# Reading every matmul's moving operand alternately from its two halves, in a float32r attention and gated-MLP kernel

## The chip, the cores and the metric

The kernel runs on one core of one Trainium2 chip. The metric is device time in microseconds, the median over runs; lower is better.

## The reference

Four sequences of 3008 tokens pass through an attention without softmax, whose result is the input of a gated MLP. Cut to what matters (the MLP's weights are float64, all else float32):

```python
scores = (1 / S) * np.matmul(z, z.transpose(0, 2, 1))      # z: 4 x 3008 x 64
attn   = np.maximum(scores, 0.0) ** 2
x      = (u * np.matmul(attn, v)).reshape(B * S, D)         # u, v: 4 x 3008 x 256
gate   = 1.0 / (1.0 + np.exp(-(x @ w_gate)))                # 256 x 1536
out    = (gate * (x @ w_val)) @ w_out                       # 1536 x 256
```

## The kernel before

All matmuls but 18 (a warm-up in bf16, L456) are in float32r: four bytes an element. To keep float32 precision each operand is held as a rounded high part and the remainder (`ah`/`al`, `vh`/`vl`, `xh`/`xl`, `hh`/`hl`, `wgv_h`/`wgv_l`, `wo_h`/`wo_l`), and a product is three matmuls into one PSUM tile: high by high, high by low, low by high. The scores do it with two, since `zP` and `zQ` hold high and low stacked over the 128 partitions.

The queries of a sequence are cut into six chunks of 512 columns, the last of 448 (3008 = 5 x 512 + 448); a chunk's columns are the moving operand of every matmul that belongs to it. The keys go in 12 pairs of 128. A step is one (sequence, chunk, pair). In a step TensorE works, in this order, on

- `pe_scores` (L260, L261) of the next step: 4 matmuls into `sc`; for a key block whose scores were computed earlier, the transposed block comes back from DRAM instead (`load_back`) and there are none;
- `pe_pv` (L330, L331, L333): 12 matmuls into `acc`, which grows over the 12 steps of a chunk;
- `pe_out` (L401 to L403): 6 matmuls into `oacc`, for the MLP of the chunk before, two feature blocks back;
- `pe_gv` (L358 to L360): 12 matmuls into `gv`, gate and value of one feature block, for the chunk before.

The step order is written out by hand in one loop (under `manual_schedule`), and every engine runs its part in that order. PSUM is full: `sc`, `gv`, `acc` and `oacc` are single tiles of two banks each.

Who reads PSUM: the Relu of `post_scores` on ScalarE (ACT, L271, followed by a square in SBUF); the Sigmoid of `gate` on ACT (L369) and the product of gate and value on VectorE (DVE, L370); `make_x` on DVE (L338), once a chunk, which multiplies `acc` by the transposed `u`; and `finish` on DVE (L408), which transposes the output in blocks of 32 by 32. Everything else that prepares a moving operand (`split`, `split_h`, `split_x`, the casts of `post_scores`) works from SBUF to SBUF.

Before the change all of these patterns are plain: a matmul reads its n columns in order, one after the other, and so do those that read its product.

Of the kernel before, what the change touches and what calls it, by code (L numbers as in the profile page):

```python
# [13 lines left out]
AF = mybir.ActivationFunctionType  # L14
ALU = mybir.AluOpType
# [13 lines left out]
def kernel(  # L29
# [19 lines left out]
    nc = tc.nc  # L49
    P = 128  # L50
# [6 lines left out]
    NF = DFF // P  # L57
    NB = D // P
    TAIL = S - (2 * NPAIR - 1) * P
    assert D == 256 and DQ == 64 and NF == NPAIR and TAIL == 64 and S % 32 == 0  # L60
    scale = 1.0 / S

    def chunk(c):
        return min(CH, S - c * CH)
# [11 lines left out]
    def f32(ap):  # L76
        return ap.bitcast(F32)


    def kept(b, c, e):  # L80
        return e > c and (b, c) not in ((0, 0), (0, 1))


    def back(b, c, k):
        return kept(b, k // 2, c)
# [159 lines left out]
    def early(b, c):  # L245
        return (b, c) == (0, 0)
# [4 lines left out]
    def pe_scores(b, c, k):  # L251
        if back(b, c, k):
            return
        n = chunk(c)
        sc = ps.tile([P, 2, CH], F32, tag="gv" if early(b, c) and k % 2 else "sc", name="sc")
        kP = z_t[b, k // 2][0]
        qP, qQ = z_t[b, c]
        for j in range(2):
            o = (k % 2) * 256 + j * P
            nc.tensor.matmul(sc[:, j, 0:n], kP[:, o : o + P], qP[:, 0:n], start=True, stop=False)  # L260
            nc.tensor.matmul(sc[:, j, 0:n], kP[:, o : o + P], qQ[:, 0:n], start=False, stop=True)  # L261
        sc_t[b, c, k] = sc

    def post_scores(b, c, k):
        n = chunk(c)
        sc = sc_t.pop((b, c, k), None)
        if back(b, c, k):
            r = r_t.pop((b, c, k))
        else:
            r = two.tile([P, 2, CH], F32, tag="r", name="r")  # L270
            nc.scalar.activation(r[:, :, 0:n], sc[:, :, 0:n], AF.Relu, scale=scale)  # L271
            nc.scalar.activation(r[:, :, 0:n], r[:, :, 0:n], AF.Square)  # L272
        if early(b, c) and k % 3 == 2:
            ah = one.tile([P, 2, CH], F32R, tag="xh", name="ah")
            al = one.tile([P, 2, CH], F32R, tag="xl", name="al")
        else:
            ah = two.tile([P, 2, CH], F32R, tag="ah", name="ah")
            al = two.tile([P, 2, CH], F32R, tag="al", name="al")
        if back(b, c, k) or (b, c) == (0, 1) or (early(b, c) and k % 2):
            nc.scalar.activation(ah[:, :, 0:n], r[:, :, 0:n], AF.Copy)  # L280
        else:
            nc.vector.tensor_copy(ah[:, :, 0:n], r[:, :, 0:n])  # L282
        nc.vector.tensor_tensor(al[:, :, 0:n], r[:, :, 0:n], f32(ah[:, :, 0:n]), op=ALU.subtract)  # L283
        a_t[b, c, k] = ah, al
        r_t[b, c, k] = r
# [30 lines left out]
    def pe_pv(b, c, k):  # L316
        n = chunk(c)
        if k == 0:
            acc_t[b, c] = ps.tile(
                [P, NB, CH], F32, tag="oacc" if early(b, c) else "acc", name="acc"  # L320
            )
        acc = acc_t[b, c]
        ah, al = a_t.pop((b, c, k))
        vh, vl = v_t[b, k]
        for j in range(2):
            last = k == NPAIR - 1 and j == 1
            for d in range(NB):
                ds = slice(d * P, (d + 1) * P)
                o = acc[:, d, 0:n]
                nc.tensor.matmul(o, vh[:, j, ds], ah[:, j, 0:n], start=(k == 0 and j == 0), stop=False)  # L330
                nc.tensor.matmul(o, vh[:, j, ds], al[:, j, 0:n], start=False, stop=last)  # L331
                if not last:
                    nc.tensor.matmul(o, vl[:, j, ds], ah[:, j, 0:n], start=False, stop=False)  # L333

    def make_x(b, c):
        n = chunk(c)
        acc, ut = acc_t.pop((b, c)), u_t[b, c]
        nc.vector.tensor_tensor(ut[:, :, 0:n], acc[:, :, 0:n], ut[:, :, 0:n], op=ALU.mult)  # L338

    def split_x(b, c):  # L340
        n = chunk(c)
# [6 lines left out]
    gv_t, h_t, oacc_t = {}, {}, {}  # L348

    def pe_gv(b, c, f, tag="gv"):  # L350
        n = chunk(c)
        gv = ps.tile([P, 2, CH], F32, tag=tag, name="gv")
        xh, xl = x_t[b, c]
        for i in range(2):
            o = gv[:, i, 0:n]
            for d in range(NB):
                wh, wl = wgv_h[:, f, i, d, :], wgv_l[:, f, i, d, :]
                nc.tensor.matmul(o, wh, xh[:, d, 0:n], start=(d == 0), stop=False)  # L358
                nc.tensor.matmul(o, wh, xl[:, d, 0:n], start=False, stop=False)  # L359
                nc.tensor.matmul(o, wl, xh[:, d, 0:n], start=False, stop=(d == NB - 1))  # L360
        gv_t[b, c, f] = gv

    g_t = {}
# [1 line left out]
    def gate(b, c, f):  # L365
        n = chunk(c)
        gv = gv_t.pop((b, c, f))
        g = one.tile([P, CH], F32, tag="g", name="g")
        nc.scalar.activation(g[:, 0:n], gv[:, 0, 0:n], AF.Sigmoid)  # L369
        nc.vector.tensor_tensor(g[:, 0:n], gv[:, 1, 0:n], g[:, 0:n], op=ALU.mult)  # L370
        g_t[b, c, f] = g


# [11 lines left out]
    def pe_out(b, c, f):  # L385
        if f == 0:
            t = ps.tile([P, NB, CH], F32, tag="oacc", name="oacc")
            oacc_t[b, c] = [t[:, h] for h in range(NB)]
        for h in range(NB):
            pe_out_half(b, c, f, h)  # L390
        if f == NF - 1:
            osb = two.tile([P, NB, CH // 32, 32], F32, tag="osb", name="osb")
            for h in range(NB):
                finish(b, c, h, osb[:, h])

    def pe_out_half(b, c, f, h):
        n = chunk(c)
        hh, hl = h_t[b, c, f]
        wh, wl = (w[:, f, h * P : (h + 1) * P] for w in (wo_h, wo_l))
        o = oacc_t[b, c][h][:, 0:n]  # L400
        nc.tensor.matmul(o, wh, hh[:, 0:n], start=(f == 0), stop=False)  # L401
        nc.tensor.matmul(o, wh, hl[:, 0:n], start=False, stop=False)  # L402
        nc.tensor.matmul(o, wl, hh[:, 0:n], start=False, stop=(f == NF - 1))  # L403

    def finish(b, c, h, osb):
        n = chunk(c)
        rows = out[b * S + c * CH : b * S + c * CH + n, :]
        nc.vector.transpose(  # L408
            out=osb[:, 0 : n // 32, :].rearrange("p T d -> p (T d)"),
            in_=oacc_t[b, c][h][:, 0:n],  # L410
        )
        for g in range(4):
            d0 = h * P + 32 * g
            nc.sync.dma_start(
                rows[:, d0 : d0 + 32].rearrange("(T p) d -> p T d", p=32),
                osb[32 * g : 32 * g + 32, 0 : n // 32, :],
            )
# [26 lines left out]
    with tc.manual_schedule():  # L444
# [19 lines left out]
        load_v(0, 1)  # L464
        keep_warm(14)
        pe_scores(*steps[0])
        turn_z(0, 1)
        prep_z(0, 1)
        load_z(0, 3)
        post_scores(*steps[0])  # L470
        pe_scores(*steps[1])
        prep_v(0, 0)
        load_v(0, 2)
        post_scores(*steps[1])
        prep_v(0, 1)
        load_v(0, 3)
# [6 lines left out]
        for g, (b, c, k) in enumerate(steps):  # L483
# [3 lines left out]
            if nxt:  # L487
                pe_scores(*nxt)
            if m1:
                gate(*m1)  # L490
            if k == 0 and C > 0:
                split_x(*chunks[C - 1])
            if nxt:
                post_scores(*nxt)
# [14 lines left out]
            if nxt:  # L509
                turn(*nxt)  # L510
            pe_pv(b, c, k)
            if k == (9 if C < 2 else 6):
                load_u(b, c)
            if k == (10 if C < 2 else 8):
                prep_u(b, c)
            if k == NPAIR - 1:
                make_x(b, c)
# [3 lines left out]
            if C > 0:  # L521
                m1 = (*chunks[C - 1], k)
                pe_gv(*m1)
# [16 lines left out]

        last = chunks[-1]
        gate(*m1)
        split_x(*last)
        split_h(*m1)
# [3 lines left out]
        def out_half(f, h):  # L548
            if f == 0:
                t = ps.tile([P, CH], F32, tag=("oacc", "acc")[h], name="oacc")  # L550
                oacc_t.setdefault(last, []).append(t)
            pe_out_half(*last, f, h)
            if f == NF - 1:
                finish(*last, h, two.tile([P, CH // 32, 32], F32, tag="osb", name="osb"))

        for f in range(NF):
            pe_gv(*last, f, tag=("sc", "gv")[f % 2])
            if m1:
                gate(*m1)
                split_h(*m1)  # L560
            if m2:
                if m2[:2] == last:
                    out_half(m2[2], 0)
                else:
                    pe_out(*m2)
            m1, m2 = (*last, f), m1
# [37 lines left out]
```

## Time and profile before

| | |
|---|---|
| median of 3 runs | 2133.43 us (2132.82 to 2134.42) |
| span of the profiled execution | 2132.2 us |
| PE (TensorE matmul) busy | 2103.2 us, 99%, 9354 matmuls |
| PEld (weight loads, beside PE) | 1758.8 us, 82% |
| DVE busy | 1176.6 us, 55% |
| ACT busy | 900.8 us, 42% |
| DMA | 159.86 MB, mean 75 GB/s |
| mean granted TensorE clock | 0.995 of full |

The profiled execution's own time is read as its span; the median of the runs lies 1.2 us above it. A matmul's duration in these rows runs from its start to the end of its drain and overlaps the next one, so the rate of TensorE is read from the distance between starts, or from a long stretch and the count of matmuls in it. A row's count stands behind an x; "idle" and the releaser behind it tell what an engine waited for.

### The profile page before, as it was taken

To read this page: it belongs to the slowest core of one execution; us is meant where nothing else is said; L and a number is where in the kernel's file an instruction comes from. 1 tells how busy PE (TensorE), PEld (TensorE's weight loads), DVE (VectorE), ACT (ScalarE), POOL (GpSimd) and SP (SyncE) were. 2 spreads that over 40 slices of the span, in tenths; PEclk is the share of its full clock that TensorE was granted. 3 is DMA by queue.
4 is the path that set the end of the run, shared out by engine and by line. 5 is a ranking of instruction groups with operands and counts; after the bars stand their busy time and mean duration, and the time that the engine had idled before them with its cause. 6 is when DMAs were issued, how large, how long until landed. Compare 5 with 4: busy or idle time off the path is not lost.

```text
span 2132.2 us, 24546 instructions
## 1 busy us (share of the span) xinstructions
PE 2103.2 (99%) x9354; PEld 1758.8 (82%) x9354; DVE 1176.6 (55%) x1557; ACT 900.8 (42%) x1202; POOL 68.9 (3%) x57
## 2 busy tenths in 40 slices
PE   7799999999999999999999999999999999999998
PEld 5588888888888888888888888888888888888888
DVE  6886545455655464544665645445466565453543
ACT  6674434344444433334544433334444434343332
POOL 2100000001000000001100000000110000000000
PEclk9899999999999999999999999999999999999999
DMA  4321312234434242425253525142535242432311
GB/s 123 97 67 23 67 40 37 60 78 107 78 75 72 65 97 53 104 48 149 70 88 62 100 41 117 34 111 60 140 67 97 46 99 50 97 67 70 88 35 19
DMA packets 689910, 159.86 MB, mean 75 GB/s; under 512 B 640768, under 2 KB 668416, under 8 KB 689792
## 3 DMA queue, kind: packets, MB, share of 16 engines
q1 hardware_dynamic: 689792, 158.30, 34.1%
q8 instruction: 73, 1.20, 0.2%
q14 instruction: 45, 0.37, 0.1%
HBM read 88.74 MB, written 63.44 MB: 71 GB/s over the span
## 4 chain that ended last, share of the span: by engine, by line
PE 95%; DVE 2%; ACT 1%; DMA 1%; issue 0%; SPq 0%; POOL 0%; DVEq 0%; ACTq 0%
PE gv L359 12%; PE gv L360 12%; PE gv L358 12%; PE acc L330 11%; PE acc L331 11%; PE acc L333 11%; PE oacc L402 6%; PE oacc L403 6%; PE oacc L401 6%; PE sc L261 4%; PE sc L260 4%; DMA wraw<-in_moe_w_val_dram 1%; DVE al L283 0%; DVE wb L139 0%; DVE wa L135 0%
## 5 line engine op out<-in xcount | busy, mean ns | idle before, releaser
L369 ACT ACTIVATE g<-gv 128x512 f32<-128x512 f32 (+1 forms) x288 | 169.4, 588 | 1022.9 <-PE gv L360 1003.3
L370 DVE TENSOR_TENSOR g<-gv,g 128x512 f32<-128x512 f32 (+1 forms) x288 | 195.7, 680 | 570.0 <-ACT g L369 569.8
L331 PE MATMUL acc<-al,vh 128*128 128x512 f32 (+1 forms) x1152 | 446.7, 388 | 5.0 <-DVE al L283 4.9
L358 PE MATMUL gv<-xh,wgv_h 128*128 128x512 f32 (+1 forms) x1152 | 444.9, 386 | 4.2 <-ACT xh L94 4.2
L330 PE MATMUL acc<-ah,vh 128*128 128x512 f32 (+1 forms) x1152 | 446.1, 387 | 2.9 <-ACT vh L212 1.5
L359 PE MATMUL gv<-xl,wgv_h 128*128 128x512 f32 (+1 forms) x1152 | 444.6, 386 | 1.1 <-DVE xl L95 1.1
L360 PE MATMUL gv<-xh,wgv_l 128*128 128x512 f32 (+1 forms) x1152 | 444.4, 386 | 0.0
L333 PE MATMUL acc<-ah,vl 128*128 128x512 f32 (+1 forms) x1056 | 408.7, 387 | 1.3 <-POOL vl L95 1.3
L283 DVE TENSOR_TENSOR al<-r,ah 128x1024 fp32r<-128x1024 f32 (+1 forms) x288 | 351.4, 1220 | 42.3 <-ACT ah L280 33.0
L282 DVE CAST ah<-r 128x1024 fp32r<-128x1024 f32 (+1 forms) x168 | 115.8, 690 | 274.8 <-ACT r L272 274.8
L331 PEld LDWEIGHTS acc<-al,vh 128*128 128x128 f32 x1152 | 217.5, 189 | 49.4 <-DVE al L283 8.1
L330 PEld LDWEIGHTS acc<-ah,vh 128*128 128x128 f32 x1152 | 217.4, 189 | 46.2 <-ACT vh L212 1.9
L358 PEld LDWEIGHTS gv<-xh,wgv_h 128*128 128x128 f32 x1152 | 216.8, 188 | 45.8 <-ACT xh L94 5.0
L359 PEld LDWEIGHTS gv<-xl,wgv_h 128*128 128x128 f32 x1152 | 216.8, 188 | 42.2 <-DVE xl L95 1.9
L360 PEld LDWEIGHTS gv<-xh,wgv_l 128*128 128x128 f32 x1152 | 216.7, 188 | 40.5
L333 PEld LDWEIGHTS acc<-ah,vl 128*128 128x128 f32 x1056 | 199.4, 189 | 39.1 <-POOL vl L95 1.9
L402 PE MATMUL oacc<-hl,wo_h 128*128 128x512 f32 (+1 forms) x576 | 222.1, 386 | 0.0
L403 PE MATMUL oacc<-hh,wo_l 128*128 128x512 f32 (+1 forms) x576 | 221.9, 385 | 0.0
L401 PE MATMUL oacc<-hh,wo_h 128*128 128x512 f32 (+1 forms) x576 | 221.9, 385 | 0.0
L271 ACT ACTIVATE r<-sc 128x1024 f32<-128x1024 f32 (+1 forms) x186 | 189.6, 1019 | 50.5 <-PE sc L261 50.5
L95 DVE TENSOR_TENSOR hl<-g,hh 128x512 fp32r<-128x512 f32 (+1 forms) x288 | 195.7, 679 | 9.2 <-ACT hh L94 9.2
L272 ACT ACTIVATE r<-r 128x1024 f32<-128x1024 f32 (+1 forms) x186 | 195.8, 1053 | 5.9
(48 smaller groups left out, 1614.5 us busy)
## 6 DMA issues: line engine op xcount, KB each, us to landing
turned<-turned SPq DMA_DIRECT2D x780, 64.0 KB, 1.9
r<-turned SPq DMA_DIRECT2D x66, 512.0 KB, 4.0
r<-turned SPq DMA_DIRECT2D x36, 448.0 KB, 3.9
vraw<-in_v_dram SPq DMA_DIRECT2D x44, 256.0 KB, 3.0
uraw<-in_u_dram SPq DMA_DIRECT2D x160, 64.0 KB, 2.5
out_dram<-osb SPq DMA_DIRECT2D x160, 64.0 KB, 1.9
wraw<-in_moe_w_gate_dram SPq DMA_DIRECT2D x12, 256.0 KB, 2.8
wraw<-in_moe_w_val_dram SPq DMA_DIRECT2D x12, 256.0 KB, 3.1
```

The source lines that it names most:

```text
L95: (eng or nc.vector).tensor_tensor(lo, src, f32(hi), op=ALU.subtract)
L272: nc.scalar.activation(r[:, :, 0:n], r[:, :, 0:n], AF.Square)
L283: nc.vector.tensor_tensor(al[:, :, 0:n], r[:, :, 0:n], f32(ah[:, :, 0:n]), op=ALU.subtract)
L330: nc.tensor.matmul(o, vh[:, j, ds], ah[:, j, 0:n], start=(k == 0 and j == 0), stop=False)
L331: nc.tensor.matmul(o, vh[:, j, ds], al[:, j, 0:n], start=False, stop=last)
L333: nc.tensor.matmul(o, vl[:, j, ds], ah[:, j, 0:n], start=False, stop=False)
L358: nc.tensor.matmul(o, wh, xh[:, d, 0:n], start=(d == 0), stop=False)
L359: nc.tensor.matmul(o, wh, xl[:, d, 0:n], start=False, stop=False)
L360: nc.tensor.matmul(o, wl, xh[:, d, 0:n], start=False, stop=(d == NB - 1))
L401: nc.tensor.matmul(o, wh, hh[:, 0:n], start=(f == 0), stop=False)
L402: nc.tensor.matmul(o, wh, hl[:, 0:n], start=False, stop=False)
L403: nc.tensor.matmul(o, wl, hh[:, 0:n], start=False, stop=(f == NF - 1))
```

## The change

Every moving operand is read through `moving`: of n columns, first column 0, then column n/2, then 1, then n/2 + 1, and so on. With float32r and n = 512 two successive reads lie 1024 bytes apart, and two reads of the same half 4 bytes. The stationary operands and the order in which the product is written to PSUM (one column after the other) stay. The products thus lie in PSUM with their columns shuffled, and each of the five readers of PSUM takes them with a step of two columns (8 bytes), first the even places, then the odd ones, and writes them in order. The number of instructions and their order on each engine are as before: 9354 matmuls of the same shapes.

```diff
--- before.py
+++ after.py
@@ -76,6 +76,23 @@
     def f32(ap):
         return ap.bitcast(F32)
 
+
+    def moving(ap):
+
+        return ap.rearrange("p (t n) -> p n t", t=2)
+
+    def product(ap):
+
+        return ap.rearrange("p (n t) -> p t n", t=2)
+
+    def products(ap):
+        return ap.rearrange("p j (n t) -> p j t n", t=2)
+
+    def by_half(ap):
+        return ap.rearrange("p (t n) -> p t n", t=2)
+
+    def by_halves(ap):
+        return ap.rearrange("p j (t n) -> p j t n", t=2)
 
     def kept(b, c, e):
         return e > c and (b, c) not in ((0, 0), (0, 1))
@@ -257,8 +274,8 @@
         qP, qQ = z_t[b, c]
         for j in range(2):
             o = (k % 2) * 256 + j * P
-            nc.tensor.matmul(sc[:, j, 0:n], kP[:, o : o + P], qP[:, 0:n], start=True, stop=False)
-            nc.tensor.matmul(sc[:, j, 0:n], kP[:, o : o + P], qQ[:, 0:n], start=False, stop=True)
+            nc.tensor.matmul(sc[:, j, 0:n], kP[:, o : o + P], moving(qP[:, 0:n]), start=True, stop=False)
+            nc.tensor.matmul(sc[:, j, 0:n], kP[:, o : o + P], moving(qQ[:, 0:n]), start=False, stop=True)
         sc_t[b, c, k] = sc
 
     def post_scores(b, c, k):
@@ -268,7 +285,7 @@
             r = r_t.pop((b, c, k))
         else:
             r = two.tile([P, 2, CH], F32, tag="r", name="r")
-            nc.scalar.activation(r[:, :, 0:n], sc[:, :, 0:n], AF.Relu, scale=scale)
+            nc.scalar.activation(by_halves(r[:, :, 0:n]), products(sc[:, :, 0:n]), AF.Relu, scale=scale)
             nc.scalar.activation(r[:, :, 0:n], r[:, :, 0:n], AF.Square)
         if early(b, c) and k % 3 == 2:
             ah = one.tile([P, 2, CH], F32R, tag="xh", name="ah")
@@ -327,15 +344,16 @@
             for d in range(NB):
                 ds = slice(d * P, (d + 1) * P)
                 o = acc[:, d, 0:n]
-                nc.tensor.matmul(o, vh[:, j, ds], ah[:, j, 0:n], start=(k == 0 and j == 0), stop=False)
-                nc.tensor.matmul(o, vh[:, j, ds], al[:, j, 0:n], start=False, stop=last)
+                nc.tensor.matmul(o, vh[:, j, ds], moving(ah[:, j, 0:n]), start=(k == 0 and j == 0), stop=False)
+                nc.tensor.matmul(o, vh[:, j, ds], moving(al[:, j, 0:n]), start=False, stop=last)
                 if not last:
-                    nc.tensor.matmul(o, vl[:, j, ds], ah[:, j, 0:n], start=False, stop=False)
+                    nc.tensor.matmul(o, vl[:, j, ds], moving(ah[:, j, 0:n]), start=False, stop=False)
 
     def make_x(b, c):
         n = chunk(c)
         acc, ut = acc_t.pop((b, c)), u_t[b, c]
-        nc.vector.tensor_tensor(ut[:, :, 0:n], acc[:, :, 0:n], ut[:, :, 0:n], op=ALU.mult)
+        x = by_halves(ut[:, :, 0:n])
+        nc.vector.tensor_tensor(x, products(acc[:, :, 0:n]), x, op=ALU.mult)
 
     def split_x(b, c):
         n = chunk(c)
@@ -355,9 +373,9 @@
             o = gv[:, i, 0:n]
             for d in range(NB):
                 wh, wl = wgv_h[:, f, i, d, :], wgv_l[:, f, i, d, :]
-                nc.tensor.matmul(o, wh, xh[:, d, 0:n], start=(d == 0), stop=False)
-                nc.tensor.matmul(o, wh, xl[:, d, 0:n], start=False, stop=False)
-                nc.tensor.matmul(o, wl, xh[:, d, 0:n], start=False, stop=(d == NB - 1))
+                nc.tensor.matmul(o, wh, moving(xh[:, d, 0:n]), start=(d == 0), stop=False)
+                nc.tensor.matmul(o, wh, moving(xl[:, d, 0:n]), start=False, stop=False)
+                nc.tensor.matmul(o, wl, moving(xh[:, d, 0:n]), start=False, stop=(d == NB - 1))
         gv_t[b, c, f] = gv
 
     g_t = {}
@@ -366,8 +384,9 @@
         n = chunk(c)
         gv = gv_t.pop((b, c, f))
         g = one.tile([P, CH], F32, tag="g", name="g")
-        nc.scalar.activation(g[:, 0:n], gv[:, 0, 0:n], AF.Sigmoid)
-        nc.vector.tensor_tensor(g[:, 0:n], gv[:, 1, 0:n], g[:, 0:n], op=ALU.mult)
+        gh = by_half(g[:, 0:n])
+        nc.scalar.activation(gh, product(gv[:, 0, 0:n]), AF.Sigmoid)
+        nc.vector.tensor_tensor(gh, product(gv[:, 1, 0:n]), gh, op=ALU.mult)
         g_t[b, c, f] = g
 
 
@@ -398,16 +417,16 @@
         hh, hl = h_t[b, c, f]
         wh, wl = (w[:, f, h * P : (h + 1) * P] for w in (wo_h, wo_l))
         o = oacc_t[b, c][h][:, 0:n]
-        nc.tensor.matmul(o, wh, hh[:, 0:n], start=(f == 0), stop=False)
-        nc.tensor.matmul(o, wh, hl[:, 0:n], start=False, stop=False)
-        nc.tensor.matmul(o, wl, hh[:, 0:n], start=False, stop=(f == NF - 1))
+        nc.tensor.matmul(o, wh, moving(hh[:, 0:n]), start=(f == 0), stop=False)
+        nc.tensor.matmul(o, wh, moving(hl[:, 0:n]), start=False, stop=False)
+        nc.tensor.matmul(o, wl, moving(hh[:, 0:n]), start=False, stop=(f == NF - 1))
 
     def finish(b, c, h, osb):
         n = chunk(c)
         rows = out[b * S + c * CH : b * S + c * CH + n, :]
         nc.vector.transpose(
             out=osb[:, 0 : n // 32, :].rearrange("p T d -> p (T d)"),
-            in_=oacc_t[b, c][h][:, 0:n],
+            in_=product(oacc_t[b, c][h][:, 0:n]),
         )
         for g in range(4):
             d0 = h * P + 32 * g
```

## Rows read from the trace of the kernel before

**Rows 1.** The page, part 1: busy time, share of the span, instructions of each engine.

```profile
span 2132.2 us, 24546 instructions
...
PE 2103.2 (99%) x9354; PEld 1758.8 (82%) x9354; DVE 1176.6 (55%) x1557; ACT 900.8 (42%) x1202; POOL 68.9 (3%) x57
```

**Rows 2.** Windows over the whole span: stretch, length, each engine's busy time (count), clock.

```profile
0.00:95.00 95.00, 71.66 (x247) 49.34 (x248) 71.76 (x94) 58.95 (x74) 20.12 (x18) 0.89 0.43 112
95.00:2127.50 2032.50, 2031.56 (x9109) 1709.47 (x9107) 1104.23 (x1464) 841.82 (x1129) 48.78 (x39) 1.00 0.34 73
2127.50:2132.20 4.70, 0.00 (x0) 0.00 (x0) 0.59 (x1) 0.00 (x0) 0.00 (x0) 0.84 0.29 49
```

**Rows 3.** Windows: one stretch of 512-column matmuls alone, one of 448-column alone.

```profile
627.96:966.16 338.20, 338.20 (x1493) 280.12 (x1492) 177.49 (x230) 128.60 (x168) 0.00 (x0) 1.00 0.35 75
...
2086.00:2127.00 41.00, 41.00 (x204) 38.01 (x203) 16.86 (x27) 12.94 (x23) 0.00 (x0) 1.00 0.11 19
```

**Rows 4.** Timeline, PE: bf16 warm-up matmuls; start, us, what.

```profile
5.06 0.81 PE L456 MATMUL warm<-idle 128*128 128x512 bf16 x3
...
8.83 0.39 PE L456 MATMUL warm<-idle 128*128 128x512 bf16 x1
```

**Rows 5.** Timeline, PE: float32r matmuls between 90 and 92 us.

```profile
90.06 0.63 PE L358 MATMUL gv<-xh,wgv_h 128*128 128x512 f32 x1
90.49 0.63 PE L359 MATMUL gv<-xl,wgv_h 128*128 128x512 f32 x1
...
91.34 0.63 PE L358 MATMUL gv<-xh,wgv_h 128*128 128x512 f32 x1
```

**Rows 6.** Windows: the stretch around them, with the granted clock.

```profile
86.20:93.00 6.80, 4.75 (x10) 3.42 (x11) 4.34 (x7) 4.66 (x5) 0.00 (x0) 0.50 0.20 73
```

**Rows 7.** Lines by form: a weight load, and 448-column matmuls of two lines.

```profile
L359 PEld LDWEIGHTS gv<-xl,wgv_h 128*128 128x128 f32 x1152 | 216.8, 188 | 42.2 <-DVE xl L95 1.9
...
L359 PE MATMUL gv<-xl,wgv_h 128*128 128x448 f32 x192 | 70.3, 366 | 0.7 <-DVE xl L95 0.7
...
L402 PE MATMUL oacc<-hl,wo_h 128*128 128x448 f32 x96 | 35.2, 366 | 0.0
```

**Rows 8.** Lines by form: the five that read PSUM; two ACT reads of SBUF.

```profile
L271 ACT ACTIVATE r<-sc 128x1024 f32<-128x1024 f32 x174 | 178.6, 1026 | 48.6 <-PE sc L261 48.6
...
L369 ACT ACTIVATE g<-gv 128x512 f32<-128x512 f32 x240 | 143.3, 597 | 878.4 <-PE gv L360 878.4
...
L370 DVE TENSOR_TENSOR g<-gv,g 128x512 f32<-128x512 f32 x240 | 165.9, 691 | 526.0 <-ACT g L369 525.9
...
L338 DVE TENSOR_TENSOR ut<-acc,ut 128x1024 f32<-128x1024 f32 x20 | 24.4, 1218 | 0.0
...
L408 DVE STREAM_TRANSPOSE osb<-oacc 128x512 f32<-128x512 f32 x40 | 26.1, 692 | 11.4 <-PE oacc L403 11.4
...
L128 ACT ACTIVATE wa<-wraw 128x512 f32<-128x512 f32 x18 | 11.9, 662 | 10.8 <-DMA wraw<-in_moe_w_val_dram 10.7
...
L150 ACT ACTIVATE wgv_h<-wa 128x512 fp32r<-128x512 f32 x12 | 7.4, 620 | 5.5 <-DVE wa L142 5.5
```

**Rows 9.** Timeline, DVE: the gate's product and make_x at a chunk's end.

```profile
700.89 0.69 DVE L370 TENSOR_TENSOR g<-gv,g 128x512 f32<-128x512 f32 x1 [1.51 <-ACT g L369]
...
703.58 1.22 DVE L338 TENSOR_TENSOR ut<-acc,ut 128x1024 f32<-128x1024 f32 x1
```

**Rows 10.** Timeline, PE: when it next writes gv, and then acc.

```profile
703.68 0.39 PE L358 MATMUL gv<-xh,wgv_h 128*128 128x512 f32 x1
...
706.40 0.39 PE L330 MATMUL acc<-ah,vh 128*128 128x512 f32 x1
```

**Rows 11.** Timeline, PE: float32r matmuls in the opening.

```profile
7.67 0.40 PE L261 MATMUL sc<-zQ,zP 128*128 128x512 f32 x1
7.91 0.39 PE L260 MATMUL sc<-zP 128*128 128x512 f32 x1
```

**Rows 12.** Lines of the first 95 us: the Relu that reads the scores.

```profile
L271 ACT ACTIVATE r<-sc 128x1024 f32<-128x1024 f32 x15 | 15.1, 1007 | 0.3 <-PE sc L261 0.3
```

## The prediction

> **What bounds the kernel now.** Start with the page's part 1: PE is busy 99% of a span of 2132.2 us, DVE 55%, ACT 42% [rows 1]. A busy PE may still be a waiting or a slow one, so look next at the windows: after the first 95 us PE is busy for all but 0.9 us of 2032.5, with 9109 matmuls, at the full granted clock (1.00, that is 2.4 GHz); the first 95 us hold 247 matmuls and 23.3 us of idle, and 4.7 us follow the last matmul [rows 2]. So some 95% of the time is one uninterrupted stream of matmuls, and it shortens only if the distance between two starts does.
>
> That distance is the number to look at. In a stretch that holds 512-column matmuls alone, 338.20 us for 1492 of them make 226.7 ns each; in the tail of 448-column ones 41.00 us for 203 make 202.0 ns [rows 3]. The clock alone would ask for 512/2.4 = 213.3 and 448/2.4 = 186.7 ns. So a float32r matmul has 13.4 or 15.3 ns over its columns. Three rows tell where they are not. Bf16 matmuls of the same shape, at the full clock, need 0.81 us for three, the last of which lasts 0.39 to its drain: two gaps in 0.42 us, so 0.21 to 0.22 each, and not under 0.213 by the clock; I take 0.215 [rows 4]. Float32r matmuls at the lower level of the clock (granted 0.50) stand 0.43 us apart, which is 512/1.2 = 0.427 with nothing on top [rows 5, 6]. And a weight load lasts 188 ns and begins with the matmul before it, so it ends well ahead of 226.7, though not far ahead of 202 [rows 7]. What is left is the delivery of a four-byte moving operand at the higher clock: 512 columns in 226.7 ns, where the array could take them in 213.3. This is what the change touches. The rows don't tell whether the 13.4 ns grow with the columns (a pause now and then in the read) or are paid once per matmul.
>
> **The change, part by part.** No instruction is added, dropped or moved, so no wait and no queue changes its place; only the address patterns differ.
>
> *Moving operand of 9336 float32r matmuls (the 9354 less 18 bf16).* No row shows one read with a jump, so the price is bounded by the nearest rows. Lower end: the limit of the read goes away and a 512-column matmul comes down to the bf16 distance, 226.7 - 215 = 11.7 ns gained (213.3 would be the last end, 13.4). Upper end: two columns that don't lie side by side can't be fetched together, and the read goes at half pace, one column in 0.833 ns, which is the distance of the rows at the lower clock, 426.7 ns: 200 ns lost. I take the lower end, since the array waits for nothing else in these rows and successive reads now come from two places 1024 bytes apart, so that each of the two has twice the time for its next column; but the rows do not show that this is the cure, and both ends stay.
> Count: there are eleven matmul lines; the 448-column ones are 192 in each of five, 176 + 8 in the sixth (`vl` and `vlast`), 96 in each of three and 24 in each of two, 1480 in all (two of these counts in [rows 7]). Of the 9109 after 95 us, 7629 have 512 columns: 7629 x 11.7 ns = 89 us (102 at 13.4). The 448-column ones have their weight load close behind: between 0 and 13.5 ns (202.0 less 448 x 215/512 = 188), I take 4, as the load's 188 ns and the few after it leave little: 1480 x 4 = 6 us (0 to 20). The 247 in the first 95 us stand beside 23 us of waits for others; at most 3 us, taken as 0.
>
> *PSUM readers with a step of two columns.* They cost now 1026 ns (Relu), 597 (Sigmoid), 691 (product), 1218 (`make_x`) and 692 (output transpose) [rows 8]. The nearest strided read is ACT's L128, which takes every second float32 from SBUF: 662 ns against 620 for the plain L150 [rows 8], 7%. Ends: 0 and double. In the stream they are covered even when doubled. Where a chunk ends, the product starts at 700.89 and lasts 0.69, `make_x` starts at 703.58 and lasts 1.22 [rows 9]; PE writes `gv` again at 703.68 and `acc` at 706.40 [rows 10]. From 701.58 to 703.68 there are 2.1 us for 0.60 + 0.69 more; from 704.80 to 706.40 there are 1.6 us for 1.22 more. In that stretch DVE is busy 177.5 and ACT 128.6 of 338.2 us [rows 3], so a PE that is 5% faster overtakes neither. Not covered are the opening, with 15 Relus of 1.0 us [rows 12], and the last transpose before the end: 7% of 15.1 + 0.7 is 1 us, double 16. I take 1.
>
> Sum: 89 + 6 - 1 = 94 us less. From the span that gives 2132.2 - 94 = 2038; the median of the runs lies 1.2 us above the span, so **2039 us**.
>
> **A rule on the distance between matmuls.** By the Trainium skill, "TensorE: Matmul & The Clock Gate", section "Wait — 56ns, not 53.3ns?", start-to-start is N divided by 2.4 GHz plus about 2.5 ns once warm, 215.7 ns at 512 columns, whatever is read. The bf16 rows here agree with it; the float32r rows, at 226.7, don't. By that rule alone the present distance would already be 215.7 and this change would be worth nothing.
>
> **The rivals.**
>
> *Half pace (slower), chance 0.20.* The two columns that enter in one tick of the slower clock are fetched as a pair from one place; split over two halves they need two fetches. Place: every matmul after 95 us. Price: 7629 x 200 ns + 1480 x (373.3 - 202.0 = 171.3 ns) = 1526 + 254 = 1780 us, so about 3910. For it: the distance of 226.7 already stands above the array's, so the read has no time to spare. Against it: nothing in the trace, since no matmul in it reads with a jump. It decides as soon as a column costs more than the slack: 0.47 ns more per matmul (4.3 us over 9109) are enough for slower by over 0.2%, about what a measurement of this kernel can tell from no change.
> The Trainium skill speaks for this one: "SBUF — State Buffer", section "Door 1: The DMA port swizzle (why [64,N] ≈ [32,N])", says that SBUF has lines of 16 bytes, that at least two successive accesses must hit a line for full bandwidth, and that each crossing is penalised. In the new order every column is in another line than the one before. No run here shows it: ACT's L128 still has two hits in a line.
>
> *A small loss at PE, chance 0.13.* Jumping between the halves costs a pause now and then, as other traffic seems to in the opening, where two starts stand 0.24 us apart at 7.67 and 7.91 [rows 11]: 5 to 13 ns a matmul, 9109 x 5 to 13 = 46 to 118, so 2179 to 2252. Doubled PSUM reads alone (16 us, 2149) are its mild form.
>
> *Nothing at PE, chance 0.22.* The 13.4 ns are paid once per matmul (a start of the read, not its pace), and the read follows any pattern at this pace. Then only the 1 us of the PSUM readers is left: 2133 to 2135. That the pattern would be folded back into a plain run, so that the change does nothing, ends here too; it can't be, because two successive reads lie 1024 bytes apart.
>
> **How the numbers follow.** The forecast, faster, has 0.45: the excess is in the read of the operand and nowhere else, but its cure is not shown. The likeliest case alone runs from 2010 (213.3 ns, all of the 20 us at 448 columns, 3 us in the opening) to 2110 (a quarter of the gain). The range leaves out half pace: from 2015 to 2220 it holds 0.45 + 0.22 + most of 0.13, about 0.79. Faster 0.45, same 0.22, slower 0.33.
>
> **What would show it.** Right: in a stretch of 512-column matmuls the count per time rises from 1492 in 338 us to about 1570, PE stays at 99% with no new waits, and the Relu and the Sigmoid keep their 1026 and 597 ns within a tenth. Half right: the distance falls, but a wait for the Sigmoid, the product or `make_x` appears before `gv` or `acc`. Wrong: the distance stays at 226.7 (paid once per matmul), or rises (to about 427 if half pace holds). Were the 448-column matmuls to fall as far as the 512-column ones, my floor by the weight load was wrong.

## The result and the profile after

The changed kernel takes 2033.49 us (median of 4 runs, 2031.97 to 2034.27), the kernel before 2133.93 us beside it. The ratio is 0.9529, with a 95% interval of 0.9516 to 0.9543: 4.7% faster, 100.4 us. The forecast was 2039 us.

The page, part 1, of the changed kernel:

```profile
span 2031.2 us, 24546 instructions
...
PE 1995.7 (98%) x9354; PEld 1768.0 (87%) x9354; DVE 1178.9 (58%) x1557; ACT 901.5 (44%) x1202; POOL 68.6 (3%) x57
```

The span is 101.0 us shorter than in [rows 1], and PE's busy time 107.5. The other engines are busy for nearly the same time, and so their shares of the shorter span rise. The windows of the changed kernel answer to [rows 2] and [rows 3] (columns as there; the last two hold the same matmuls in program order as the 512-column stretch and the 448-column tail there):

```profile
0.00:95.00 95.00, 67.12 (x247) 47.49 (x248) 72.00 (x93) 59.62 (x74) 20.49 (x18) 0.91 0.41 112
95.00:2026.50 1931.50, 1928.62 (x9109) 1720.52 (x9107) 1106.36 (x1465) 841.89 (x1129) 48.16 (x39) 1.00 0.36 77
2026.50:2031.20 4.70, 0.00 (x0) 0.00 (x0) 0.56 (x1) 0.00 (x0) 0.00 (x0) 1.00 0.29 49
602.16:924.19 322.03, 322.03 (x1494) 282.00 (x1494) 177.57 (x230) 128.31 (x168) 0.00 (x0) 1.00 0.37 78
1987.81:2025.83 38.02, 38.02 (x202) 37.99 (x202) 16.84 (x27) 12.89 (x23) 0.00 (x0) 1.00 0.12 20
```

The first 95 us hold 247 matmuls, as before: nothing is gained there, where PE waits for others. The 9109 matmuls after it take 1931.5 us instead of 2032.5, and that is the whole difference. The distance is now 322.03/1492 = 215.8 ns between 512-column matmuls instead of 226.7, and 38.02 us for 201 distances = 189.2 ns between 448-column ones instead of 202.7. (The prediction's 202.0 divides a window by 203; only 201 distances between starts lie in it, and they take 202.7 ns each, 16.0 over the clock.) Both new distances are the clock's time plus 2.5 ns (213.3 + 2.5 and 186.7 + 2.5). Idle time of PE after 95 us rises from 0.9 to 2.9 us.

Lines by form of the changed kernel, which answer to [rows 7] and [rows 8] (L288, L388, L389, L356 and L427 are the five readers of PSUM):

```profile
L377 PEld LDWEIGHTS gv<-xl,wgv_h 128*128 128x128 f32 x1152 | 218.1, 189 | 27.6 <-DVE xl L112 1.9
...
L288 ACT ACTIVATE r<-sc 128x1024 f32<-128x1024 f32 x174 | 177.7, 1021 | 41.7 <-PE sc L278 41.7
L389 DVE TENSOR_TENSOR g<-gv,g 128x512 f32<-128x512 f32 x240 | 165.5, 690 | 455.7 <-ACT g L388 455.7
...
L388 ACT ACTIVATE g<-gv 128x512 f32<-128x512 f32 x240 | 142.9, 596 | 793.3 <-PE gv L378 782.6 <-DVE wa L149 10.3
...
L427 DVE STREAM_TRANSPOSE osb<-oacc 128x512 f32<-128x512 f32 x40 | 26.1, 691 | 8.7 <-PE oacc L422 8.7
...
L356 DVE TENSOR_TENSOR ut<-acc,ut 128x1024 f32<-128x1024 f32 x20 | 24.3, 1217 | 0.0
```

Relu 1021 ns (1026 before), Sigmoid 596 (597), product 690 (691), `make_x` 1217 (1218), transpose 691 (692): a step of two columns in PSUM costs these five nothing that shows. The weight load takes 189 ns, as long as the whole distance between two 448-column matmuls.

Two of the waits of PE in the changed kernel (engine, line, for whom; us in total, times, longest):

```profile
PE gv L376 <- ACT xh L111: 6.0, 2, 5.8
...
PE gv L376 <- DVE g L389: 1.8, 4, 0.6
```

Of the first, all but 0.2 us is one wait in the opening; the second is new, 1.8 us at four of the 288 feature blocks (the third and the last of the first chunk, the fourth of two later ones), where the faster PE reaches `pe_gv` before the product has freed `gv`.

### The profile page after: what moved, and what is told of

It reads as the page before. It is cut to its first block, busy times and chain, and to the rows that moved or that the text cites. A ratio compares the mean times of both kernels' runs of the same rounds, so it can differ in the third digit from the quotient of the medians.

```text
span 2031.2 us, 24546 instructions
## 1 busy us (share of the span) xinstructions
PE 1995.7 (98%) x9354; PEld 1768.0 (87%) x9354; DVE 1178.9 (58%) x1557; ACT 901.5 (44%) x1202; POOL 68.6 (3%) x57
## 4 chain that ended last, share of the span: by engine, by line
PE 92%; DVE 3%; ACT 2%; DMA 1%; issue 1%; SPq 0%; POOL 0%; ACTq 0%; DVEq 0%
PE gv L377 12%; PE gv L376 12%; PE gv L378 12%; PE acc L347 11%; PE acc L348 11%; PE acc L350 11%; PE oacc L422 6%; PE oacc L421 6%; PE oacc L420 6%; PE sc L278 4%; PE sc L277 4%; DVE al L300 1%; DMA wraw<-in_moe_w_val_dram 0%; ACT r L289 0%; ACT r L288 0%
## 5 line engine op out<-in xcount | busy, mean ns | idle before, releaser
L388 ACT ACTIVATE g<-gv 128x512 f32<-128x512 f32 (+1 forms) x288 | 169.0, 587 | 918.7 <-PE gv L378 898.5
L389 DVE TENSOR_TENSOR g<-gv,g 128x512 f32<-128x512 f32 (+1 forms) x288 | 195.1, 677 | 483.8 <-ACT g L388 483.7
L376 PE MATMUL gv<-xh,wgv_h 128*128 128x512 f32 (+1 forms) x1152 | 433.1, 376 | 7.9 <-ACT xh L111 6.0
L348 PE MATMUL acc<-al,vh 128*128 128x512 f32 (+1 forms) x1152 | 433.8, 377 | 6.9 <-DVE al L300 6.9
L347 PE MATMUL acc<-ah,vh 128*128 128x512 f32 (+1 forms) x1152 | 433.8, 377 | 4.3 <-ACT vh L111 2.8
L377 PE MATMUL gv<-xl,wgv_h 128*128 128x512 f32 (+1 forms) x1152 | 432.6, 375 | 1.1 <-DVE xl L112 1.1
L378 PE MATMUL gv<-xh,wgv_l 128*128 128x512 f32 (+1 forms) x1152 | 432.2, 375 | 0.0
L350 PE MATMUL acc<-ah,vl 128*128 128x512 f32 (+1 forms) x1056 | 397.1, 376 | 1.3 <-POOL vl L112 1.3
L420 PE MATMUL oacc<-hh,wo_h 128*128 128x512 f32 (+1 forms) x576 | 215.8, 375 | 0.0
L421 PE MATMUL oacc<-hl,wo_h 128*128 128x512 f32 (+1 forms) x576 | 215.8, 375 | 0.0
L422 PE MATMUL oacc<-hh,wo_l 128*128 128x512 f32 (+1 forms) x576 | 215.8, 375 | 0.0
L288 ACT ACTIVATE r<-sc 128x1024 f32<-128x1024 f32 (+1 forms) x186 | 188.7, 1014 | 43.1 <-PE sc L278 42.8
```

What stands on the lines that cost most here:

```text
L347: nc.tensor.matmul(o, vh[:, j, ds], moving(ah[:, j, 0:n]), start=(k == 0 and j == 0), stop=False)
L348: nc.tensor.matmul(o, vh[:, j, ds], moving(al[:, j, 0:n]), start=False, stop=last)
L350: nc.tensor.matmul(o, vl[:, j, ds], moving(ah[:, j, 0:n]), start=False, stop=False)
L376: nc.tensor.matmul(o, wh, moving(xh[:, d, 0:n]), start=(d == 0), stop=False)
L377: nc.tensor.matmul(o, wh, moving(xl[:, d, 0:n]), start=False, stop=False)
L378: nc.tensor.matmul(o, wl, moving(xh[:, d, 0:n]), start=False, stop=(d == NB - 1))
```

## The experiments

**Patterns by themselves.** A small kernel issues forty matmuls in a row for each pattern, with the other engines idle; like the two small ones after it, it was run once. The core of it:

```python
a = m[:, 0:512]                                             # float32r, real data of u
halves     = a.rearrange("p (t n) -> p n t", t=2)           # 0, 256, 1, 257, ...
quarters   = a.rearrange("p (t n) -> p n t", t=4)
sixteenths = a.rearrange("p (t n) -> p n t", t=16)
step2      = a.rearrange("p (n t) -> p t n", t=2)           # 0, 2, 4, ..., 1, 3, 5, ...; step4, step8 alike
twos       = a.rearrange("p (t n e) -> p n t e", t=2, e=2)  # 0, 1, 256, 257, ...; fours: e=4
near8      = a.rearrange("p (n t e) -> p n e t", t=2, e=2)  # 0, 2, 1, 3, ...
near16     = a.rearrange("p (n t e) -> p n e t", t=2, e=4)  # 0, 4, 1, 5, 2, 6, 3, 7, ...; near64: e=16
for i in range(40):
    nc.tensor.matmul(acc[:, i % 2, :], w[:, i % 2, :], halves, start=True, stop=True)
...
```

> A kernel of its own: forty float32r matmuls in a row for each of several read patterns of the moving operand, all 512 columns wide and between the same two weight tiles, then plain ones of 496, 480 and 464 columns, halves at 480, and plain bf16. It computes nothing of the reference. Read is the distance between starts. All theories: plain 226.7 ns, halves 215.8, bf16 215 to 216. Place (the pause comes from a run that goes through one stretch of memory in order, and two streams far apart hide it): halves, quarters, sixteenths, far (8 KB apart), odd (1040 bytes apart), twos and fours (2 or 4 columns from each half in turn) all about 216; steps of 2, 4 or 8 columns and the near patterns (columns 8, 16 or 64 bytes apart in turn) stay at 226.7 or more. Neighbours (the pause comes from two successive reads in the same 16 bytes): halves, quarters, sixteenths, far, odd, step 4, step 8, near 16 and near 64 about 216; step 2, near 8, twos and fours stay near 226.7. Any pattern (all that is not one plain run takes another path of the address generator): everything but plain about 216. Per matmul or per column: at 496, 480 and 464 columns plain stands 13.4 ns above the clock's 206.7, 200.0 and 193.3 if it is paid once, 13.0, 12.5 and 12.1 if it grows with the columns.

Windows of this kernel, one for each pattern, from its first start to its last (39 distances), all at the full granted clock. In order: plain, halves, quarters, sixteenths, step 2, step 4, twos, fours, near 8, near 16, plain of 480 columns, halves of 480:

```profile
25.86:34.93 9.07, 9.07 (x41) 7.48 (x40) 0.00 (x0) 0.00 (x0) 0.00 (x0) 1.00 0.01 2
35.16:43.57 8.41, 8.41 (x40) 7.37 (x39) 0.00 (x0) 0.00 (x0) 0.00 (x0) 1.00 0.00 0
43.79:54.83 11.04, 11.04 (x41) 7.48 (x39) 0.00 (x0) 0.00 (x0) 0.00 (x0) 1.00 0.00 0
55.11:72.05 16.94, 16.94 (x40) 8.04 (x39) 0.00 (x0) 0.00 (x0) 0.00 (x0) 1.00 0.00 1
72.49:90.09 17.60, 17.60 (x40) 8.10 (x39) 0.00 (x0) 0.00 (x0) 0.00 (x0) 1.00 0.00 0
90.55:108.53 17.98, 17.98 (x40) 8.12 (x39) 0.00 (x0) 0.00 (x0) 0.00 (x0) 1.00 0.00 0
...
126.25:139.51 13.26, 13.26 (x41) 7.71 (x39) 0.00 (x0) 0.00 (x0) 0.00 (x0) 1.00 0.00 0
139.85:149.61 9.76, 9.76 (x40) 7.38 (x39) 0.00 (x0) 0.00 (x0) 0.00 (x0) 1.00 0.00 0
149.86:158.74 8.88, 8.88 (x40) 7.32 (x39) 0.00 (x0) 0.00 (x0) 0.00 (x0) 1.00 0.01 2
158.97:167.39 8.42, 8.42 (x41) 7.37 (x40) 0.00 (x0) 0.00 (x0) 0.00 (x0) 1.00 0.00 0
...
202.44:210.90 8.46, 8.46 (x41) 7.31 (x40) 0.00 (x0) 0.00 (x0) 0.00 (x0) 1.00 0.00 0
...
219.52:227.41 7.89, 7.89 (x40) 7.37 (x39) 0.00 (x0) 0.00 (x0) 0.00 (x0) 1.00 0.00 0
```

Divided by 39, in the order of the rows: 232.6, 215.6, 283, 434, 451, 461, 340, 250, 228, 215.9, 216.9 and 202.3 ns. Plain, the control, has one distance of 425 and eight of 224 to 236 at its start and then 226.7; near 8 too begins with nine unsettled ones and then has 226.7. Step 8 took 431, and near 64, far (8 KB apart) and odd (1040 bytes apart) 215.8. Plain matmuls of 496, 480 and 464 columns stand 16.5 to 17.0 ns over the clock, which neither of the two expectations (13.4, or 12.1 to 13.0) has. No theory survives as it stood. "Place" falls with near 16: two streams 16 bytes apart do as well as two 8 KB apart. "Neighbours" falls with the quarters, the sixteenths and the steps of 4 and 8, which never read two columns of the same 16 bytes in succession and are slower than plain. "Any pattern" falls with the same rows. Half pace and worse exist (step 4: 461 ns), but not for halves.

What the numbers do suggest is to count by every other column. Take every other column that a matmul reads (the first, third, fifth) as one stream and those between as another. In halves and near 16 each stream finds four columns in a row in a 16-byte line; in plain and near 8 two; in the steps and sixteenths one. Four: 215.8 ns. Two: 227. One: 431 to 461. Quarters and twos also have one, and cost less (283 and 340). This became the theory of the next round, lines.

**Lines.** The second small kernel tests it with bf16 (whose element is two bytes) and with streams that skip:

```python
b_step2   = mb[:, 0:1024].rearrange("p (n t) -> p n t", t=2)[:, :, 0]        # bf16, every 4 bytes
b_step4   = mb.rearrange("p (n t) -> p n t", t=4)[:, :, 0]                   # bf16, every 8 bytes
b_halves2 = mb[:, 0:1024].rearrange("p (t n e) -> p n t e", t=2, e=2)[:, :, :, 0]
halves2   = m[:, 0:1024].rearrange("p (t n e) -> p n t e", t=2, e=2)[:, :, :, 0]
halves4   = m[:, 0:2048].rearrange("p (t n e) -> p n t e", t=2, e=4)[:, :, :, 0]
jump4     = m.rearrange("p (n y t e) -> p n y e t", y=8, t=2, e=4)[:, :, 0]
jump2     = m.rearrange("p (n y t e) -> p n y e t", y=4, t=2, e=4)[:, :, 0, 0:2]
```

> A second kernel of patterns, forty matmuls in a row of each (it computes nothing of the reference). The theory after the first, call it lines: the odd and the even columns of a matmul are fetched by two streams, each with one line of 16 bytes open, and the pace hangs on how many columns in a row a stream finds in its line: four cost nothing, two (plain float32r) come a little late, one runs at about half pace. Rival width: it is the four-byte element of float32r that costs. Rival places: it is the two places far apart that help. Bf16 with a step of two columns (4 bytes) has the addresses of plain float32r: lines 227, width 216; with a step of four columns (8 bytes): lines 430 to 460, width 216; halves with a step of two: 216 by both. Float32r, halves with a step of two columns in each: lines 227 (two in a row), places 216; halves with a step of four: lines 430 to 460, places 216; two neighbouring lines read in turn and then a jump of 256 bytes: lines 216, places more; the same with two columns of each line and a jump of 128 bytes: lines 227 to 250. If bf16 with a step of two does cost, its narrower ones tell how: at 384, 256 and 128 columns plain bf16 stands at 162, 109 and 56; with the step 173, 120 and 67 if the cost is paid once per matmul, 171, 115 and 59 if it grows with the columns.

Its windows, 39 distances each, in order: bf16 with a step of two, with a step of four, halves with a step of two; bf16 plain at 256 columns, with the step at 256, plain at 128, with the step at 128; float32r halves with a step of two, with a step of four, jump after four of each line, jump after two:

```profile
37.14:45.94 8.80, 8.80 (x39) 3.72 (x39) 0.00 (x0) 0.00 (x0) 0.00 (x0) 1.00 0.00 0
46.17:63.76 17.59, 17.32 (x39) 4.49 (x39) 0.00 (x0) 0.00 (x0) 0.00 (x0) 1.00 0.00 0
64.22:85.29 21.07, 21.07 (x40) 3.88 (x39) 0.00 (x0) 0.00 (x0) 0.00 (x0) 1.00 0.00 1
...
99.14:103.39 4.25, 4.25 (x40) 3.81 (x39) 0.00 (x0) 0.00 (x0) 0.00 (x0) 1.00 0.01 4
103.50:107.92 4.42, 4.42 (x41) 3.75 (x39) 0.00 (x0) 0.00 (x0) 0.00 (x0) 1.00 0.00 0
108.04:110.21 2.17, 2.17 (x41) 2.17 (x39) 0.00 (x0) 0.00 (x0) 0.00 (x0) 1.00 0.00 0
110.27:112.52 2.25, 2.25 (x42) 2.25 (x40) 0.00 (x0) 0.00 (x0) 0.00 (x0) 1.00 0.00 0
...
130.38:139.24 8.86, 8.86 (x41) 7.32 (x39) 0.00 (x0) 0.00 (x0) 0.00 (x0) 1.00 0.00 0
139.47:157.12 17.65, 17.65 (x40) 8.07 (x39) 0.00 (x0) 0.00 (x0) 0.00 (x0) 1.00 0.00 1
157.58:166.01 8.43, 8.43 (x41) 7.38 (x39) 0.00 (x0) 0.00 (x0) 0.00 (x0) 1.00 0.00 0
166.23:174.68 8.45, 8.45 (x40) 7.30 (x39) 0.00 (x0) 0.00 (x0) 0.00 (x0) 1.00 0.00 0
```

Bf16 with a step of two costs 225.6 ns by its window, 225.9 between its starts, against 215.8 plain: the addresses of plain float32r bring its price, so width falls. The step of four costs 451. Float32r halves with a step of two (two in a row) cost 227, with a step of four (one in a row) 453, four of a line and then a jump 216: as lines said, and places falls again (it had 216 for the first two). The narrower bf16 ones tell that the cost is a pace: with the step they are slower by 10.1 ns at 512 columns, 7.6 at 384, (4.42 - 4.25)/39 = 4.4 at 256 and 2.1 at 128. In bf16 it grows with the columns; it is not paid once per matmul.

Two values missed. Bf16 halves with a step of two were to cost 216 and cost 540, although they are read at the very byte distances of float32r halves. And two of a line with a jump of 128 bytes were to cost 227 to 250 and cost 216.7.

**Bf16 and mixtures.** The third small kernel asks whether bf16 has one stream only, and what plain and halves do to each other:

```python
b_halves = b.rearrange("p (t n) -> p n t", t=2)              # bf16: 0, 256, 1, 257, ...
b_near16 = b.rearrange("p (n t e) -> p n e t", t=2, e=8)
b_eights = b.rearrange("p (t n e) -> p n t e", t=2, e=8)     # eight of each half; eights alike in float32r
near32   = a.rearrange("p (n t e) -> p n e t", t=2, e=8)
for i in range(40):
    nc.tensor.matmul(acc[:, i % 2, :], w[:, i % 2, :], a, start=True, stop=True)
    nc.tensor.matmul(acc[:, i % 2, :], w[:, i % 2, :], halves, start=True, stop=True)
...
```

> A third kernel of patterns (it computes nothing of the reference), after two surprises: bf16 read in halves with a step of two took 540 ns, and e4_mlp_only gained 46 us instead of 56. Two theories of the first: bf16 has one stream where float32r has two (one stream), so bf16 in halves, and bf16 from two neighbouring lines in turn, finds a new line for every column: some 540 ns each, while eight columns from each half in turn (a whole line) stay at 216. Or the step of two was to blame: both 216. Float32r, eight columns from each half in turn: two in a row per stream and line, so 227 to 250; from two lines 32 bytes apart in turn: 216. Of the second: plain and halves in turn, one each, and eight plain then eight halves. If a plain matmul costs the same wherever it starts: 226.7 after each plain one, 215.8 after each of the halves. If its cost hangs on when it starts: 224 to 236 after a plain one, as in e4_mlp_only, whose plain matmuls are spread over these values.

Its windows, in order: bf16 halves, bf16 near 16, bf16 eights, float32r eights, and plain and halves in turn (39 distances, of pairs in the last):

```profile
36.76:55.65 18.89, 18.89 (x40) 3.82 (x39) 0.00 (x0) 0.00 (x0) 0.00 (x0) 1.00 0.00 0
56.14:75.07 18.93, 18.93 (x40) 3.81 (x39) 0.00 (x0) 0.00 (x0) 0.00 (x0) 1.00 0.00 0
75.56:83.97 8.41, 8.41 (x40) 3.82 (x39) 0.00 (x0) 0.00 (x0) 0.00 (x0) 1.00 0.01 2
...
101.94:111.42 9.48, 9.48 (x40) 7.42 (x39) 0.00 (x0) 0.00 (x0) 0.00 (x0) 1.00 0.01 2
...
120.31:137.72 17.41, 17.41 (x79) 14.65 (x78) 0.00 (x0) 0.00 (x0) 0.00 (x0) 1.00 0.00 0
```

Bf16 in halves costs 484 ns, in near 16 as much (485), and in eights 215.6: bf16 behaves as if it had one stream, to which the alternation brings a new line with each column. The size is not explained: 540 were expected, and a new line for each column costs 540 with the step of two and 484 without. And if bf16 has one stream, its steps in the second kernel did not test two: counted so, eight columns in a row cost 215.8 ns, four 225.9, two 451. Counted over all columns, plain float32r (four in a row, 226.7) and its step of two (two, 451) have these same prices; it is the patterns that alternate between lines which set float32r apart. Float32r eights cost 243, near 32 215.9, both within what lines said. In turn, a pair takes 17.41/39 = 446.4 ns: the halves stand 215 ns from the next start, and the plain ones 231 or 232 instead of 226.7. After eight halves the first plain one costs 238, the next 231 or 232, and from the fourth on 227. So a plain matmul's cost does hang on what stands before it, as in the first nine plain ones of the first kernel.

**The readers of PSUM plain again.** The matmuls stay in halves:

```diff
     def product(ap):
-        return ap.rearrange("p (n t) -> p t n", t=2)
+        return ap
 
     def products(ap):
-        return ap.rearrange("p j (n t) -> p j t n", t=2)
+        return ap
...
```

> The changed kernel with its five readers of PSUM plain again: the matmuls read in halves, the products stay with their columns out of order, and nothing puts them back (this part of the computation is left out). If the readers' step of two columns costs nothing, as their rows say (1021 and 596 ns), this is within 0.1% of the changed kernel, 2033 us. If it costs in the opening and at the chunk ends, this is up to 6 us faster, and the waits at the chunk ends (some 6 us more in all than before the change) shrink.

2033.33 us, ratio 0.9529 (0.9513 to 0.9545): the same as the changed kernel. Putting the columns in order costs nothing that shows. Nor do the new waits come from it: after 95 us PE waits 2.7 us in the changed kernel and 2.9 here (0.9 before the change; most of the 6 us of the text above lie in the opening).

**The other half alone.** The readers keep their step, the matmuls are plain:

```diff
     def moving(ap):
-        return ap.rearrange("p (t n) -> p n t", t=2)
+        return ap
```

> The other half alone: the matmuls read plainly as before, the five readers of PSUM take their columns with a step of two, so the columns come out of order (this part of the computation is wrong by that). If the whole gain is TensorE's read: 2133 to 2135 us, the matmuls 226.7 ns apart. If a part of the gain came from the readers: below 2129.

2133.58 us, ratio 0.9999 (0.9989 to 1.0008). The 512-column stretch:

```profile
627.44:965.65 338.21, 338.21 (x1494) 280.03 (x1492) 177.48 (x230) 128.59 (x168) 0.00 (x0) 1.00 0.35 75
```

The matmuls stand 338.21/1492 = 226.7 ns apart again. All of the gain is TensorE's read.

**Halves in the MLP alone.** `moving` is taken out of `pe_scores` and `pe_pv`, and the Relu and `make_x` read plainly:

```diff
-                nc.tensor.matmul(o, vh[:, j, ds], moving(ah[:, j, 0:n]), start=(k == 0 and j == 0), stop=False)
-                nc.tensor.matmul(o, vh[:, j, ds], moving(al[:, j, 0:n]), start=False, stop=last)
+                nc.tensor.matmul(o, vh[:, j, ds], ah[:, j, 0:n], start=(k == 0 and j == 0), stop=False)
+                nc.tensor.matmul(o, vh[:, j, ds], al[:, j, 0:n], start=False, stop=last)
...
```

> Halves in the MLP alone (pe_gv and pe_out with their readers), plain in pe_scores and pe_pv. The MLP has 5184 of the 9336 float32r matmuls. If each matmul gains by itself, whatever its neighbour on the engine reads, 5184 of 9336 of the 100.4 us are gained, 56 us: 2078, with 216 ns after an MLP matmul and 227 after one of the attention. If the gain needs a stream of its kind, or the pause moves on to the next plain matmul, it is clearly less.

2088.18 us, ratio 0.9788 (0.9773 to 0.9803): 46 us gained, not 56. The timeline of PE shows where the rest is; from the first row to the second stand 12 plain matmuls of `pe_pv`, from the second to the third 6 of `pe_out` in halves:

```profile
706.64 0.40 PE L347 MATMUL acc<-ah,vh 128*128 128x512 f32 x1
...
709.41 0.38 PE L420 MATMUL oacc<-hh,wo_h 128*128 128x512 f32 x1
...
710.71 0.38 PE L376 MATMUL gv<-xh,wgv_h 128*128 128x512 f32 x1
```

2.77 us for 12 are 231 ns each, 1.30 us for 6 are 217. Between starts after 95 us, the 3934 plain matmuls stand farther apart than in the kernel before, by 3.3 ns at 512 columns and 3.9 at 448, some 13 us in all, and the 5172 of the MLP closer by 11.1 and 13.4, some 59 us. The difference is the 46 us that were measured. The cost that a plain matmul takes on beside halves is thus seen in place.

**Sixteen bytes apart.** In the whole kernel, with the readers plain:

```diff
     def moving(ap):
-        return ap.rearrange("p (t n) -> p n t", t=2)
+        return ap.rearrange("p (n t e) -> p n e t", t=2, e=4)
...
```

> The changed kernel with the two columns that are read in turn only 16 bytes apart instead of half an operand (0, 4, 1, 5, 2, 6, 3, 7, then 8, 12 and so on); the readers of PSUM are plain, as in e2_readers_plain, so the columns are not put back in order. Lines: the same as e2_readers_plain, 2033 within 0.1%. Places: the gain is lost, 2133.

2032.86 us, ratio 0.953 (0.9514 to 0.9546), and in the 512-column stretch the same 322.02 us as with halves:

```profile
601.53:923.55 322.02, 322.02 (x1493) 282.09 (x1493) 177.54 (x230) 128.38 (x168) 0.00 (x0) 1.00 0.37 78
```

This is the whole gain. Halves are not needed; two neighbouring lines are enough.

**Quarters.** In the whole kernel, with the readers plain:

```diff
     def moving(ap):
-        return ap.rearrange("p (t n) -> p n t", t=2)
+        return ap.rearrange("p (t n) -> p n t", t=4)
...
```

> The changed kernel reading in turn from four quarters instead of two halves, the readers of PSUM plain (columns not put back in order). Lines: the even columns then come from the first and third quarter in turn and find a new line each time; with the 283 ns of the first pattern kernel, 56 ns more than plain for 7629 matmuls and some 46 for 1480 narrower ones, about 2630 us. If more places in turn were as good as two: 2033.

2607 us (two runs, 2599 and 2615), ratio 1.222 (1.218 to 1.227). The 512-column stretch and the 448-column tail, by the windows of this kernel:

```profile
737.95:1160.68 422.73, 422.73 (x1493) 286.46 (x1492) 176.62 (x229) 128.46 (x168) 0.00 (x0) 1.00 0.28 60
2544.04:2591.83 47.79, 47.79 (x202) 38.05 (x201) 16.81 (x27) 12.91 (x23) 0.00 (x0) 1.00 0.10 16
```

422.73/1492 = 283 ns, as in the small kernel; the 448-column ones, at 47.79/201 = 238 ns, cost 35 ns more than plain and not the 46 expected. Four places in turn lose 22% where two gain 5%.

No pattern beat halves: at 215.8 ns a matmul stands 2.5 ns over the clock's 213.3, and near 16 ties.

## Why the prediction was right, step by step

- *The excess is in the read of the operand, and it goes.* Right. 11.7 ns were expected at 512 columns, 226.7 - 215.8 = 10.9 came: 7629 x 10.9 = 83 us for 89. I read the bf16 distance as 215 ns; it is 215.8. The Trainium skill, "TensorE: Matmul & The Clock Gate", section "Wait — 56ns, not 53.3ns?", gives 215.7 ns for 512 columns; the float32r rows now agree, where before they stood 11 ns higher. (That section calls the 2.5 ns a fixed cost per matmul, hence the prediction's "whatever is read"; it names no element type.)
- *The 448-column matmuls come down by 4 ns only.* Wrong, the one term mis-sized. I took the weight load of 188 ns and "the few after it" as a floor. There are no few after it: the load takes 189 ns and the next matmul starts 189.2 ns after the last, which is the clock's time plus the same 2.5 ns as at 512 columns. Whether the load would hold up a narrower matmul, no run shows. They came down by 13 ns: 1480 x 13 = 19 us for 6, at the top of the 0 to 20 that were kept open.
- *The readers cost 1 us.* They cost none that shows (e3: ratio 0.9999). *No other engine is overtaken.* Nearly: 2 us of new waits, most of them for the product, which the prediction had listed as the sign of being half right.
- Sum: 83 + 19 - 2 = 100, against 101.0 in the span and 100.4 in the medians; 94 were forecast. Two terms were off in opposite directions (6 us too much at 512 columns, 13 too little at 448), so the sum is closer than its parts.
- *Why it would go.* The reason given, that two places 1024 bytes apart leave each twice the time for its next column, does not hold as it stands: 16 bytes apart do as well (e6), 1040 bytes or 8 KB add nothing, and four places, which leave each four times the time, cost 283 ns (e7). In this the forecast was lucky, and it had said that the cure was not shown. What orders the float32r times, as far as these patterns go, is how many columns in a row each of two streams finds in its 16-byte line (e1, e5, e8). The two streams are inferred from these times; no row shows them.
- *Half pace.* It did not come for halves, and its reason, pairs fetched from one place, is refuted: halves and near 16 split every pair and are the fastest. A pace near its 426.7 ns does exist, in other patterns: 431 to 461 ns for steps and sixteenths, and 484 for bf16 in halves. The Trainium skill, "SBUF — State Buffer", section "Door 1: The DMA port swizzle (why [64,N] ≈ [32,N])", asks for at least two successive hits in a 16-byte line. Counted over all columns of a matmul, the trace disagrees: halves never hit twice and are the fastest. Counted by every other column of float32r, it agrees in kind: one hit is slow (283 to 461), two are near full pace (216.7 to 250), and four are free. Counted over all columns of bf16, two hits are only half pace (451) and four nearly full (225.9), so there two do not suffice.
- *A small loss at PE.* It did not come for halves; eights (243) and fours (250) have such a loss. The 0.24 us of [rows 11], put down to other traffic, need none: by the trace these plain starts stand 229 to 235 ns apart, and the first kernel has 224 to 236 for its first plain ones with the other engines idle.
- *Nothing at PE, paid once per matmul.* Refuted for the kernel: the order of the read alone took away 10.9 of the 13.4 ns. On bf16 with the same addresses the excess grows with the columns (2.1 ns at 128, 10.1 at 512). In float32r, from 448 to 512 columns, it does neither: plain stands over halves by 13.5 ns at 448, 14.5 at 480 and 10.9 at 512.

So it is shown that the order in which TensorE reads the moving operand is the cause of the gain; why this order is cheaper is a theory. What stays open: lines orders the patterns but does not size them all. Quarters (283), twos (340), fours (250) and eights (243) lie between its values, and a jump of 128 bytes after two of a line is nearly free (216.7). Why float32r should have two streams and bf16 one, why plain widths between 448 and 496 stand 16 to 17 ns over the clock instead of 13.4, and why a plain matmul costs up to 238 ns after others was measured or inferred and not explained.

## What to carry to other kernels

Compare the distance between matmul starts with columns over the granted clock, not PE's busy share: here 99% busy hid 13 ns in every 227. In float32r, read two 16-byte lines in turn, column by column; with halves the readers of PSUM can undo the order with a step of two, which cost them nothing that shows here. Do it in all matmuls of a stream, since plain ones among them get slower. Do not carry it to bf16, which took 484 ns instead of 216, nor to more than two places; float32r narrower than 448 columns was not measured.

## What the runs showed of the hardware that was not expected

- Float32r and bf16 react oppositely to the same byte addresses: 1024 bytes apart in turn, with 4 bytes between the columns of a half, float32r takes 215.8 ns and bf16 540.
- Bf16 read with a step of 4 bytes has the pace of plain float32r (225.9 against 226.7 ns), and with a step of 8 bytes that of float32r with a step of two columns (451 both).
- In the kernel before, plain float32r at the full clock stands 13.4 ns over the clock's time at 512 columns and 16.0 at 448; at half the clock it stands at 0.43 us, the clock's own 0.427 as near as the rows tell [rows 5, 6].
